# Retention and GELU MLP on one core: TensorE's order of work planned around its instruction pieces

## The chip, the core and the metric

The kernel runs on one NeuronCore of a Trainium2 chip. A core has a matrix engine (TensorE, in the profile PE, with its weight loads as PEld), a vector engine (VectorE, DVE), a scalar engine (ScalarE, ACT), GpSimd (POOL, here mostly the issuer of loads) and SyncE (SP, here the issuer of stores). Each follows its own list of instructions and waits for others by semaphores. The metric is the device time of one execution in microseconds (us); smaller is better.

## What is computed

The reference is a retention layer (attention with a decay in place of the softmax) and, on its output, an MLP with the exact GELU. Inputs are float32, the output is float32.

```python
# q, k, v: (8, 8, 576, 64)
scores = q @ k.T / sqrt(64)
gamma = 1 - 2.0 ** (-5 - arange(8))                 # one decay per head
ret = scores * where(rel >= 0, gamma ** rel, 0)     # rel = row - column
x = (ret @ v).transpose(0, 2, 1, 3).reshape(4608, 512)
h = x @ w_in                                        # w_in (512, 2048)
g = 0.5 * h * (1 + erf(h / sqrt(2)))
out = g @ w_out                                     # w_out (2048, 512)
```

## The kernel before

**Attention.** The decay lets the sequence be cut into chunks of 128 rows (the last has 64). Within a chunk the scores are computed in full and masked; what earlier chunks give comes from a running state per head, the sum of scaled keys times values. A *unit* is one chunk of one batch; there are 32 full ones and four that hold the 64-row ends of two batches each. Units 0 to 3 stand alone, later full units go two to a *group* (same chunk of two batches). For a group TensorE computes the scores (L559; L547 for units 0 to 3), VectorE masks them (L592), and then comes the *visit*: TensorE multiplies the masked scores with the values (`inner`, L646, or L631 for the short ones), updates the state (`state`, L661) and adds the state's part (`cross`, L711). Each of these is 32 small products, 64 instructions with their weight loads. VectorE scales the result and writes it to `x` (L735), which is the MLP's input. Two groups with the same chunk index can be visited together ("AA" in the loop), with 64 products each. Queries and keys of the first groups are turned by TensorE (L488, L494), later ones by VectorE (L514) with a copy by ScalarE (L525). The scaled values `vh` are made by VectorE for units 0 to 3 (L613) and by ScalarE for all others (L609, `VH_ACT`).

**MLP.** Four units make a block of 512 tokens, `t` = 0 to 8. The *first products* (x times w_in) are `mlp1` (L758): in block 0 over 128 or 256 tokens as the slices of w_in (eight, `wi0` to `wi7`) land, in block 1 over 256, then over 512. From block 6 on they are done as seven half-size products of a 2 x 2 scheme of Strassen's kind (`mlp1_fast`, L972, names "h"). The *second products* (g times w_out) are plain for half of block 0 (`mlp2`, L791) and seven half-size products for the rest (`mlp2_fast`, L862, names "f"). The sums that the schemes need are VectorE's (L817, L830, L931, L950).

**Order.** The order on each engine is written by a planner in Python when the program is built: it keeps an estimated clock `T` per engine, expected landings of loads (`sw_dma`, `share`) and times at which PSUM banks and buffers come free, and takes, in each step of its main loop (L1237 to L1345), the first due thing: a visit (A, AA), a state update (U), scores (S), a turn (T), else first or second products (`mlps`), whichever block is behind. When TensorE would wait early in the run, it issues products of zeros (`warm`, L1193). `fire` (L1156) gives VectorE, ScalarE and GpSimd their work as the clock advances: `side_jobs` holds VectorE's choices by due time, with weights such as `PER_G` and `PER_B`. `pe` (L442) advances TensorE's clock; it knows durations and changes of tiling, and nothing of how instructions arrive.

**Loads** go through one GpSimd queue in the order of the string `ORDER` (L374: `wi` and `wo` are slices of w_in and w_out, `q`, `k`, `v`, `n` those of a unit, `n` being keys in another layout, `io` the constants, `dq` a decay table) and after that by `reload`, as buffers come free. **Stores** go through SP (L1190); `STORE_AT` is when the planner thinks that block 0's begin, and `CROWD` until when it counts a store as a delay of loads.

**Names of the change.** `VISIT` and `LEAD` say from which group on, and with how much attention work ahead of the MLP, two visits are tied together (L1261); `SB` how far VectorE may be behind for scores to be issued (L1277); `AHEAD` and `RATE` how far scores run ahead of the MLP (L1221); `STATE10` from when the state of units 2 and 3 may be updated; `SLACK` how near VectorE must be to idle to get a side job.

Of the kernel before, what the change touches and what calls it, by code (L numbers as in the profile page):

```python
# [17 lines left out]
def kernel(  # L18
# [14 lines left out]
    nc = tc.nc  # L33
# [47 lines left out]
    VH_POOL = 30  # L81
# [21 lines left out]
    MSK_AT = 28.0  # L103
# [337 lines left out]

    def pe(dur, to="full"):  # L442
# [38 lines left out]
    def turn(n, jj):  # L481

        qk = loaded[groups[n][0]][0][jj]
        if n < 4:
            b, t = bank([128, HP, 128], BF16, "qk_ps")
            dst, m = turned(n, jj), HP
            for x in range(HP):
                nc.tensor.transpose(t[:, x], qk[:, 2 * x:2 * x + 2, :], ident1)  # L488
        else:
            b, t = bank([128, H, 128], BF16, "qk_ps")  # L490
            dst, m = turned(n, 1) if jj else qk.rearrange("p (h s) -> p h s", h=H), H
            for y in range(2):
                for hp in range(HP):
                    nc.tensor.transpose(t[:, y * HP + hp], qk[:, 4 * D * hp + y:4 * D * hp + 4 * D:2], ident1)  # L494
# [44 lines left out]
    def scores(n):  # L539
        g = groups[n]  # L540
        if n < 4:
            qT, kT = turned(n, 0), turned(n, 1)
            got = bank_pair(128)
            for hp in range(HP):
                for e in range(2):
                    sl = slice(64 * e, 64 * e + 64)
                    nc.tensor.matmul(got[1][:, e, hp, :], lhsT=kT[sl, hp, :], rhs=qT[sl, hp, :],  # L547
                                     start=True, stop=True)
            st[g[0]]["sc"] = got, pe(0.23, "row")
        else:  # L550
            short = len(g) == 1
            got = [bank_pair(TAIL if short else C) for _ in g]
            for hp in range(HP):
                for y in range(2):
                    for e in range(2):
                        for j in range(2):
                            sl = slice(64 * e + 32 * j, 64 * e + 32 * j + 32)
                            dst = got[0][1][64 * j:64 * j + 64, e, hp, :] if short else got[j][1][:, e, hp, :]
                            nc.tensor.matmul(dst, lhsT=turned_k(n, sl, hp, y), rhs=turned_q(n, sl, hp, y),  # L559
# [62 lines left out]
    def inner(i):  # L622
        bp, ci, j = units[i]
        s = st[i]
        if j is None:
            s["o"] = o = bank_pair(TAIL)
            for h in range(H):
                for jj in range(2):
                    sl, e = slice(64 * jj, 64 * jj + 64), 64 * (h % 2)
                    y = h // 2 + HP * (h % 2)  # L630
                    nc.tensor.matmul(o[1][e:e + 64, jj, h // 2, :], lhsT=s["vh"][sl, h, :], rhs=s["ret"][y // HP][sl, y % HP, :],  # L631
# [3 lines left out]
        else:  # L635
# [7 lines left out]
            for hp in range(HP):  # L643
                for z in range(4):
                    e, d0 = z // 2, z % 2 * 32
                    nc.tensor.matmul(o[32 * z:32 * z + 32, hp, :], lhsT=vals[:, 2 * hp + e, d0:d0 + 32], rhs=s["ret"][e][:, hp, :],  # L646
# [5 lines left out]
    def state(bp, ci):  # L652
        pair = pair_of[bp, ci]
        b, u_ps = bank([128, H, D], FP32, "u_ps")
        for hp in range(HP):
            for y in range(2):
                for e in range(2):
                    for j, i in enumerate(pair):
                        h, p0 = 2 * hp + e, 64 * e + 32 * j
                        keys = loaded[i][0][1][:, h, y::2] if i < 4 else loaded[i][2][:, j, h, y::2]  # L660
                        nc.tensor.matmul(u_ps[p0:p0 + 32, 2 * hp + y, :], lhsT=keys, rhs=st[i]["vh"][:, h, :],  # L661
# [37 lines left out]
    def cross(n):  # L699
# [6 lines left out]
        for hp in range(HP):  # L706
            for y in range(2):
                for e in range(2):
                    for j in range(2):
                        sl = slice(64 * e + 32 * j, 64 * e + 32 * j + 32)  # L710
                        nc.tensor.matmul(o[64 * e:64 * e + 64, j, hp, :], lhsT=u[sl, 2 * hp + y, :], rhs=turned_q(n, sl, hp, y),  # L711
# [42 lines left out]
    def mlp1(t, m0, n, lo, hi):  # L754
        b, hT = bank([128, n, hi - lo], FP32, "hT")
        for m in range(m0, m0 + n):
            for cc in range(N_DM):
                nc.tensor.matmul(hT[:, m - m0, :], lhsT=w_in[:, cc, m * 128:m * 128 + 128], rhs=x_tiles[t][:, cc, lo:hi],  # L758
# [26 lines left out]
    def mlp2(t, ts, m0, m1):  # L785
# [4 lines left out]
        for m in range(m0, m1):  # L790
            nc.tensor.matmul(oT, lhsT=g_of(t, ts // 2)[:, m, cols], rhs=w_out[:, m, :], start=(m == 0), stop=(m == N_DF - 1))  # L791
# [59 lines left out]
    def mlp2_fast(t, p, name):  # L851
# [9 lines left out]
        for kk in range(HK):  # L861
            nc.tensor.matmul(dst, lhsT=x[:, kk, :], rhs=y[:, kk, :], start=(name in "125" and kk == 0),  # L862
# [92 lines left out]
    def mlp1_fast(t, i, name):  # L955
# [13 lines left out]
        for m in range(2):  # L969
            for cc in range(HC):  # L970
                c0 = (2 * i + m) * 128
                nc.tensor.matmul(dst[:, m, :], lhsT=a[cc][:, c0:c0 + 128], rhs=y[:, cc, :],  # L972
# [118 lines left out]
    half = 0  # L1091
    u_due = []
# [37 lines left out]
    def side_jobs(now):  # L1130
# [12 lines left out]
        if nT in BY_DVE and nT < gA + N_TK and (half or len(apart_due) < N_TQ) and all(land.get(("qk"[half], i), 1e9) + 0.1 <= now for i in groups[nT]):  # L1143
# [49 lines left out]
    def warm(n):  # L1193
        b, t = bank([128, 512], FP32, "warm")
        for _ in range(n):
            nc.tensor.matmul(t, lhsT=zeros[:, :128], rhs=zeros, start=True, stop=True)
# [21 lines left out]
    def s_ready():  # L1218
        n = group_of[nA]
        g = groups[n]  # L1220
        if n < nT and n not in [x[0] for x in apart_due] and g[-1] // 4 <= tM1 + N_XB - 1 and nA + len(g) <= AHEAD + RATE * b1:  # L1221
# [157 lines left out]
```

## Time and profile before

| what | us |
|---|---|
| median of three runs | 292.38 (292.13 to 296.99) |
| the profiled execution: its own time | 292.46 |
| its span, first to last instruction | 290.7 |
| TensorE busy with products | 278.6 |
| VectorE, ScalarE, GpSimd busy | 228.5, 180.1, 136.0 |
| the end of block 0's first products on TensorE | 33.22 |
| first half-size first product of block 6 | 201.22 |
| TensorE's last product ends | 287.0 |

The span leaves 1.76 us of the execution outside. Rows of the profile name an engine, a line of the kernel, an operation, the tile that is written and those read, a count, busy time and the idle time before it with what ended it; "issue" means that the engine waited for nothing that the profile shows. A timeline row gives its start and its length from there; products overlap a little at their ends, so durations are best taken from start to start. The queue named "instruction" is a DMA queue, with 32 packets of 16 KB. Product records can be missing: 4155 of 4179 are there.

### The profile page before, as it was taken

What the parts mean: (1) busy time and instruction counts of PE and PEld (TensorE: products, weight loads), DVE (VectorE), ACT (ScalarE), POOL (GpSimd) and SP (SyncE); (2) the same over time, 40 slices, a digit from 0 to 9 for tenths busy, and PEclk for the clock granted to TensorE, in tenths of its full rate; (3) what the DMA queues carried; (4) which work ended last, traced back from release to release, by engine and by line L of the source; (5) the groups of instructions that cost most, each with busy time, mean ns of one, the idle gap of its engine ahead of it and who ended that gap; (6) DMA issues with size and microseconds to landing.
All of it is one profiled execution on the core that took longest, in us unless ns stands there. A gap on an engine that the chain in (4) does not pass through costs nothing.

```text
span 290.7 us, 9754 instructions
## 1 busy us (share of the span) xinstructions
PE 278.6 (96%) x4155; PEld 212.4 (73%) x4179; DVE 228.5 (79%) x380; ACT 180.1 (62%) x407; POOL 136.0 (47%) x205
## 2 busy tenths in 40 slices
PE   6999998999999999999999999999999999999994
PEld 2478766888747666665767666767888888888884
DVE  6474387896969579878996888988996998899861
ACT  7456558479779587678578596744545445555421
POOL 8956867889799777775887750000000000000000
PEclk9999999999999999999999999999999999999999
DMA  9999999999989999999999980202020202101114
GB/s 154 170 188 191 196 154 205 183 135 140 141 112 100 135 144 135 190 134 190 120 109 196 98 128 3 57 19 77 0 74 0 76 0 76 72 2 72 38 54 127
DMA packets 109131, 31.96 MB, mean 110 GB/s; under 512 B 85792, under 2 KB 104736, under 8 KB 109088
## 3 DMA queue, kind: packets, MB, share of 16 engines
q0 software_dynamic: 100400, 21.12, 83.0%
q1 hardware_dynamic: 7264, 9.51, 9.9%
q10 hardware_dynamic: 1424, 0.72, 0.9%
q8 instruction: 32, 0.52, 0.7%
q14 instruction: 11, 0.09, 0.1%
HBM read 42.99 MB, written 9.44 MB: 180 GB/s over the span
## 4 chain that ended last, share of the span: by engine, by line
PE 88%; DMA 6%; POOL 3%; issue 2%; DVE 0%; POOLq 0%
PE psum L862 36%; PE psum L758 26%; PE psum L972 13%; DMA early<-in_v_dram 3%; PE psum L559 3%; PE psum L711 3%; PE psum L646 3%; PE psum L791 2%; DMA w_in<-in_moe_w_in_dram 2%; POOL early L364 2%; PE psum L661 1%; POOL w_in L307 1%; PE psum L494 1%; PE psum L631 0%; DVE vh L613 0%
## 5 line engine op out<-in xcount | busy, mean ns | idle before, releaser
L758 PE MATMUL psum<-x,w_in 128*128 128x512 bf16 (+2 forms) x547 | 90.2, 308 | 2.7 <-issue 2.0
L758 PEld LDWEIGHTS <-w_in 128*128 128x128 bf16 x568 | 49.7, 98 | 24.1 <-issue 0.8
L862 PEld LDWEIGHTS <-g_all 128*128 128x128 bf16 x544 | 52.3, 98 | 11.4 <-issue 0.7
L763 ACT ACTIVATE g_all<-psum 128x512 bf16<-128x512 f32 x64 | 37.6, 595 | 27.3 <-PE psum L758 27.3
L862 PE MATMUL psum<-w_out,g_all 128*128 128x256 bf16 x408 | 52.0, 273 | 0.5 <-issue 0.5
L862 PEld LDWEIGHTS <-s 128*128 128x128 bf16 x408 | 39.5, 98 | 8.8
L342 POOL DMA_DIRECT2D k_ld<-in_k_dram x64 | 35.1, 569 | 21.6 <-DMA kn_ld<-in_k_dram 9.7
L609 ACT ACTIVATE vh<-v_ld,dv 128x128 bf16<-128x128 bf16 (+1 forms) x144 | 42.2, 380 | 0.0
L977 ACT ACTIVATE g_all<-t 128x512 bf16<-128x512 f32 x36 | 22.6, 630 | 29.1 <-DVE t L985 29.0
L592 DVE TENSOR_TENSOR ret<-psum,msk 128x1024 bf16<-128x1024 f32 (+1 forms) x32 | 35.7, 1150 | 4.9 <-PE psum L559 4.5
L342 POOL DMA_DIRECT2D q_ld<-in_q_dram x64 | 35.1, 568 | 2.3 <-DMA q_ld<-in_q_dram 1.4
L862 PE MATMUL psum<-wt,s 128*128 128x256 bf16 x272 | 34.1, 273 | 0.0
L848 DVE TENSOR_TENSOR o_sb<-psum,t 128x256 f32<-128x256 f32 x51 | 21.5, 421 | 13.8 <-PE psum L862 6.3
L453 ACT COPY t<-psum 128x256 f32<-128x256 f32 (+1 forms) x46 | 20.0, 434 | 17.1 <-PE psum L862 13.4
L985 DVE TENSOR_TENSOR t<-psum,t 128x512 f32<-128x512 f32 x36 | 24.7, 689 | 6.0 <-ACT t L453 4.2
L766 ACT ACTIVATE g_all<-psum 128x512 bf16<-128x512 f32 (+1 forms) x39 | 19.1, 523 | 11.2 <-PE psum L758 10.7
L972 PE MATMUL psum<-x,w_in 128*128 128x256 bf16 x192 | 25.9, 273 | 0.0
L451 DVE COPY t<-psum 128x512 f32<-128x512 f32 (+1 forms) x41 | 22.7, 559 | 3.7 <-PE psum L862 3.6
L735 DVE TENSOR_TENSOR x<-psum,dqT 128x1024 bf16<-128x1024 f32 (+1 forms) x18 | 19.3, 1099 | 2.2 <-PE psum L711 2.2
L972 PEld LDWEIGHTS <-w_in 128*128 128x128 bf16 x192 | 18.8, 98 | 2.4
L972 PE MATMUL psum<-x,ws 128*128 128x256 bf16 x144 | 19.5, 273 | 0.0
L830 DVE TENSOR_TENSOR s<-g_all 128x1024 bf16<-128x1024 bf16 x17 | 12.4, 727 | 7.4 <-ACT g_all L766 6.0
(107 smaller groups left out, 374.0 us busy)
## 6 DMA issues: line engine op xcount, KB each, us to landing
out_dram<-o_sb SPq DMA_DIRECT2D x31, 256.0 KB, 2.5
v_ld<-in_v_dram POOLq DMA_DIRECT2D x14, 256.0 KB, 5.2
q_ld<-in_q_dram POOLq DMA_DIRECT2D x48, 64.0 KB, 5.5
k_ld<-in_k_dram POOLq DMA_DIRECT2D x48, 64.0 KB, 4.5
kn_ld<-in_k_dram POOLq DMA_DIRECT2D x12, 256.0 KB, 6.5
w_in<-in_moe_w_in_dram POOLq DMA_DIRECT2D x8, 256.0 KB, 8.4
w_out<-in_moe_w_out_dram POOLq DMA_DIRECT2D x8, 256.0 KB, 9.5
q_ld<-in_q_dram POOLq DMA_DIRECT2D x4, 128.0 KB, 9.3
```

Of the source, the lines that this page charges most:

```text
L342: nc.gpsimd.dma_start(qk["qk".index(what)][p0:p0 + 32, 0:HP * per].rearrange("p (h x) -> p h x", h=HP), {"q": q, "k": k}[what][2 * bp + jj ...
L451: nc.vector.tensor_copy(dst, src)
L453: nc.scalar.copy(dst, src)
L592: nc.vector.tensor_tensor(both.rearrange("p (e h) s -> p e h s", e=2), t, by, op=ALU.mult)
L609: nc.scalar.activation(vh[:, 0:m, h], src[:, :, h], AF.Copy, scale=dv[:, h, ci:ci + 1])
L758: nc.tensor.matmul(hT[:, m - m0, :], lhsT=w_in[:, cc, m * 128:m * 128 + 128], rhs=x_tiles[t][:, cc, lo:hi], start=(cc == 0), stop=(cc == N ...
L763: nc.scalar.activation(g_all[:, t % 2, :, m0, :], hT.rearrange("p n (a c) -> p (n a) c", a=2), AF.Gelu)
L848: nc.vector.tensor_tensor(dst, src, f[key], op=ALU.add)
L862: nc.tensor.matmul(dst, lhsT=x[:, kk, :], rhs=y[:, kk, :], start=(name in "125" and kk == 0), stop=(kk == HK - 1), skip_group_check=True)
L972: nc.tensor.matmul(dst[:, m, :], lhsT=a[cc][:, c0:c0 + 128], rhs=y[:, cc, :], start=(name in "125" and m == 0 and cc == 0), stop=(cc == HC ...
L977: nc.scalar.activation(g_of(t, part)[:, m0:m0 + 2], src, AF.Gelu)
L985: nc.vector.tensor_tensor(f[key], f["b"][1], f[key], op=ALU.add)
```

## The change

TensorE's instructions are counted as they are written (`mm` and `mm_turn` stand in the place of the calls for products and turns, two instructions each). `place` says in which piece of 256 a count falls, and where in it. The planner's clock waits at the end of a piece until `FETCH`, 5 us, after the piece before was entered. `fetch_at` gives a visit or a block of scores that would cross the end of a piece the time at which the next one is expected, and the main loop doesn't take it before; two visits are tied together only if they fit into two pieces (`one_piece`). Until then other products are taken.

Products of zeros are issued until 24 us of the planner's clock, for waits over 0.5 us after 16. Half-size first products no longer ask that all groups be turned, only that all loads be issued (and, as before, that their buffers be free); turning by VectorE asks for a free buffer in the ring. Several of the planner's constants and the order of loads are other ones. `JOIN` and `JOIN_SB` are zero, so `after_a` has no effect. `VH_POOL` doesn't count in either kernel, since `VH_ACT` covers all groups from 4 on.

In the programs that are built, TensorE's products are the same but for two things: 19 products of zeros (L1196 before) for 12, and 64 products of 128 columns with 224 of 256 in blocks 0 and 1 for 112 with 200. The first products of blocks 6 to 8 and the second products from block 5 on stand in the same order. Visits stand elsewhere: that of units 8 and 9 stands ahead of seven groups of first products, a block of scores and two groups of second products that it followed before, and those of units 16 and 17 and of units 18 to 21 are no longer tied. Loads: `v3` comes two slices of w_in earlier, `q4` comes later, with two slices of w_out behind it instead of seven. SP's list of stores has the same length, and GpSimd's list the same loads.

```diff
-    AHEAD = 14
-    RATE = 3.8
-    STORE_AT = 0.0
-    CROWD = 40.0
-    STATE10 = 20.0
+    AHEAD = 13
+    RATE = 4.6
+    STORE_AT = 62.0
+    CROWD = 66.0
+    STATE10 = 32.0
     HOT = 7.5
+    FETCH = 5.0
     ARRIVE = 5.6
     WPLUS = 0
-    VISIT = 8
-    LEAD = 2.0
+    WARM_TO = 24.0
+    JOIN = 0
+    JOIN_SB = 0.0
+    VISIT = 4
+    LEAD = 5.0
     NEAR = 0.6
-    SLACK, SB, PER_G, PER_B, TURN0 = 1.2, 9.0, 6.0, 40.0, 0.0
+    SLACK, SB, PER_G, PER_B, TURN0 = 1.2, 2.0, 8.0, 20.0, 0.0
...
-    ORDER = ("wi0 io k2 q1 k1 wi7 q2 v1 k3 wi1 wo2 v0 wi6 q3 v2 wi5 wi3 wi2 v3 q4 wi4 wo1 wo0 wo4 wo7 wo6 wo3 wo5 "
-             "k4 q5 v4 k5 q6 dq2 k6 k7 q7 v6 q8 q9 k8 n4 n8 k9 q10 v8 q11 dq3 n6 k11 q12 k10 v10 n10 q13 k13 dq4 "
-             "n12 k12 v12 dq0").split()
+    ORDER = ("wi0 io q1 k2 k1 wi7 v1 q2 k3 v0 wi1 wi6 q3 wo2 v2 wi5 v3 wi3 wi4 wo1 wi2 wo3 wo0 wo4 wo5 k4 q4 wo7 "
+             "q5 wo6 v4 dq2 k5 q6 k7 k6 q7 q8 q9 n4 v6 k8 k9 v8 q10 k11 n8 n6 k10 dq3 q11 q12 v10 dq0 q13 dq4 k12 "
+             "k13 n10 n12 v12").split()
...
+    count = [3.0, 3.0]
+    piece = [0.0]
+
+    def mm(*a, **k):
+        count[0] += 2.004
+        nc.tensor.matmul(*a, **k)
...
+    def place(n):
+        return (n - 194.0) // 256, (n - 194.0) % 256
+
+    def fetch_at(n):
+
+        at = place(count[0])[1]
+        wait = piece[0] + FETCH - (256 - at) * 0.0075 if at + n >= 256 else 0.0
+        return 0.0 if T["pe"] < 20.0 else wait
+
+    def one_piece(n):
+        return place(count[0])[1] + n < 512
+
     def pe(dur, to="full"):
         if mode[0] != to:
             T["pe"] += 0.05 if mode[0][:4] == to[:4] == "row4" else 0.11
             mode[0] = to
-        T["pe"] += dur * (2.0 if T["pe"] < HOT else 1.0)
+        dur *= 2.0 if T["pe"] < HOT else 1.0
+        new, old = place(count[0])[0], place(count[1])[0]
+        if new > old:
+            turn_at = T["pe"] + dur * (1 - place(count[0])[1] / max(1.0, count[0] - count[1]))
+            wait = max(0.0, piece[0] + FETCH - turn_at) if T["pe"] > 20.0 else 0.0
+            piece[0] = turn_at + wait
+            T["pe"] += wait
+        count[1] = count[0]
+        T["pe"] += dur
         return T["pe"] + DRAIN
...
-        if ("f", t - 2, 0, "3") in waiting2 or nT < N_G or name == "7" and ("f", t - 2, 1, "4") in waiting2:
+        if ("f", t - 2, 0, "3") in waiting2 or not all_loaded() or name == "7" and ("f", t - 2, 1, "4") in waiting2:
...
-        if nT in BY_DVE and nT < gA + N_TK and (half or len(apart_due) < N_TQ) and all(land.get(("qk"[half], i), 1e9) + 0.1 <= now for i in groups[nT]):
+        if nT in BY_DVE and nT < gA + N_TK and ring_free("tk" if half else "tq") and all(land.get(("qk"[half], i), 1e9) + 0.1 <= now for i in groups[nT]):
...
-                if nA > groups[n + 1][-1]:
+                if nA > groups[n + 1][-1] and one_piece(384 if len(g) > 1 else 192):
                     both = max(ready, ready_for(n + 1))
-                    acts.append((max(both, free_time(len(g) > 1 and units[g[0]][1] < NCI - 1, out_pairs(n, n + 1))), "AA"))
+                    acts.append((max(both, fetch_at(384 if len(g) > 1 else 192), free_time(len(g) > 1 and units[g[0]][1] < NCI - 1, out_pairs(n, n + 1))), "AA"))
...
-                acts.append((max(ready, free_time(n < 4, out_pairs(n))), "A"))
+                acts.append((max(ready, fetch_at(192 if n >= 4 else 0), free_time(n < 4, out_pairs(n))), "A"))
...
-            if T["dve"] <= now + SB and nA - nB <= 2:
-                acts.append((max(s_ready(), free_time(0, len(g))), "S"))
+            if T["dve"] <= now + (SB + JOIN_SB if after_a else SB) and nA - nB <= 2:
+                acts.append((max(s_ready(JOIN if after_a else 0), fetch_at(64 if n >= 4 else 0), free_time(0, len(g))), "S"))
...
-        if now < 16 and gap > (0.6 if now < HOT else 0.2):
+        if now < WARM_TO and gap > (0.6 if now < HOT else 0.2 if now < 16 else 0.5):
```

More of the change, by code (lines that the diff above doesn't have):

```diff
@@ L80 @@
     N_KN = 4
-    VH_POOL = 30
+    VH_POOL = 16
     N_VH = 4
@@ L790, in mlp2 @@
         for m in range(m0, m1):
-            nc.tensor.matmul(oT, lhsT=g_of(t, ts // 2)[:, m, cols], rhs=w_out[:, m, :], start=(m == 0), stop=(m == N_DF - 1))
+            mm(oT, lhsT=g_of(t, ts // 2)[:, m, cols], rhs=w_out[:, m, :], start=(m == 0), stop=(m == N_DF - 1))
         done = pe((m1 - m0) * 0.2158)
@@ L1195, in warm @@
         for _ in range(n):
-            nc.tensor.matmul(t, lhsT=zeros[:, :128], rhs=zeros, start=True, stop=True)
+            mm(t, lhsT=zeros[:, :128], rhs=zeros, start=True, stop=True)
         pe((0.32 if T["pe"] < HOT else 0.2158) * n)
@@ L1233 @@
         b, t = bank([128, 512], FP32, "warm")
-        nc.tensor.matmul(t, lhsT=zeros[:, :128], rhs=zeros, start=True, stop=True)
+        mm(t, lhsT=zeros[:, :128], rhs=zeros, start=True, stop=True)
         release(b, 0.0)
@@ L1328 @@
             soon.append(v_land(nV) + 0.1)
-        if nT in BY_DVE and all(("qk"[half], i) in land for i in groups[nT]):
+        if nT in BY_DVE and ring_free("tk" if half else "tq") and all(("qk"[half], i) in land for i in groups[nT]):
             soon.append(max(T["dve"], max(land["qk"[half], i] for i in groups[nT]) + 0.1) + 0.01)
```

36 lines of the change are left out of this document (22 added, 14 removed).

## The prediction

> **What bounds the kernel now.** I read the page's busy rows first, then the chain of work that ended last, then TensorE's waits after 26 us, and last its timeline around each wait.
>
> ```profile
> PE 278.6 (96%) x4155; PEld 212.4 (73%) x4179; DVE 228.5 (79%) x380; ACT 180.1 (62%) x407; POOL 136.0 (47%) x205
> PE   6999998999999999999999999999999999999994
> q8 instruction: 32, 0.52, 0.7%
> ```
>
> TensorE is busy in every slice but the first and the last. [...] The chain, in order of time, splits the run:
>
> ```profile
> 8.69 6.54 DMA w_in<-in_moe_w_in_dram
> 15.51 9.76 DMA early<-in_v_dram
> 25.30 0.70 DVE vh L613
> 26.46 6.92 PE psum L758 x96
> ```
>
> Until 26 us the chain is loads; the last is the values of unit 3, landed at 25.27. From 26.46 it is TensorE almost alone. What it still waits for after 26 us:
>
> ```profile
> PE psum L758 <- issue: 2.0, 8, 0.5
> PE psum L711 <- issue: 1.4, 1, 1.4
> PE psum L862 <- issue: 0.5, 1, 0.5
> PE psum L661 <- DVE vh L613: 0.3, 1, 0.3
> ```
>
> So after 26 us no engine and no load holds TensorE up: "issue" is all. 24 product records are missing (4155 against 4179 weight loads), and a missing record looks like a 0.16 us gap, so I compared each run of products with its own rate (128 columns 0.056, 256 columns 0.109, 512 columns 0.216 us each). Four real stops are left: 1.65 us in the L711 run at 47.84, 0.59 in the L758 run at 78.96, 0.65 in the L862 run at 140.34, 0.74 in the L758 run at 164.11: **3.6 us**. Two of them:
>
> ```profile
> 47.84 0.35 PE L711 MATMUL psum<-q_ld,u_sb 32*64 32x128 bf16 x10
> 49.60 0.52 PE L711 MATMUL psum<-q_ld,u_sb 32*64 32x128 bf16 x22 [1.41 <-issue]
> ...
> 140.34 1.38 PE L862 MATMUL psum<-w_out,g_all 128*128 128x256 bf16 x11
> 142.19 0.70 PE L862 MATMUL psum<-w_out,g_all 128*128 128x256 bf16 x5 [0.48 <-issue]
> ```
>
> They cut a run in two at a place where no operand changes. Counting weight loads and products, they stop at instruction 1215, 2493, 4793 and 5561, and 194 + 256 x (4, 9, 18, 21) is 1218, 2498, 4802, 5570. In the trace's packet records the last instruction packet before each stop landed at 48.13, 78.17, 140.79 and 163.85; products resumed at 49.60, 79.90, 142.19 and 165.40, 1.4 to 1.7 us later. So a stop is a piece that isn't there. Each packet starts after TensorE enters the piece before it, 0.5 to 4.0 us later while loads run (0.85 to 1.0 us of transfer), which makes the time from entering one piece to being able to enter the next 2.6 to 6.2 us over the 22 pieces between 43 and 190 us, median 3.9, over 5 us in six.
>
> [...]
>
> **The change part by part.** The built programs' orders are known, so I can place each product.
>
> Pieces. TensorE's time from one boundary to the next follows from rows: 32 products of scores 0.56 us, inner 0.46, state 0.35, cross 0.57; in pairs (64) as here:
>
> ```profile
> 137.79 1.08 PE L646 MATMUL psum<-ret,vh 128*32 128x128 bf16 x64
> 138.69 0.70 PE L661 MATMUL psum<-vh,kn_ld 128*32 128x64 bf16 x64
> 139.32 1.08 PE L711 MATMUL psum<-q_ld,u_sb 32*64 32x128 bf16 x64
> ```
>
> that is 0.90, 0.63 and 1.02 from start to start. Before, the short pieces take 2.8, 3.8, 4.0, 4.0, 4.0, 4.2, 4.3, 4.9, 4.9, 5.4, 5.5, 5.6 us. In the new order they take 4.7, 4.9, 4.9, 5.1, 5.1, 5.3, and nine of 5.5 to 5.9: fewer products of visits stand in one piece, because the new count and test (lines 447 to 484 of the changed kernel) put a visit just behind a boundary, and MLP products between. Laying the 22 measured fetch times over the pieces of before, place by place, gives 4.5 us of stops where 3.6 were measured (0.8 of it); over the new pieces 2.4, so 1.9 with that factor. Drawing them at random gives 5.3 before (0.67) and 1.9 after, so 1.3. I take **1.6 us of stops, a gain of 2.0**; ends: none left (gain 3.6), and 3.6 as before (gain 0). A visit that waits costs TensorE nothing by itself: behind the tests stand first and second products, which are the same in sum, and no visit of before was waited for.
>
> Visits alone. VISIT 4 and LEAD 5 join other visits than before: those of units 16/17 and of 18 to 21 were joined and are now single. A single visit takes 0.46 + 0.35 + 0.57 = 1.38 us, a joined one 2.55 for two: **+0.25** for the two splits with the short one at the smaller sizes (bounds 0 and 0.4).
>
> The first 40 us. Seven more products of zeros (19 against 12) and another order of loads. What one costs:
>
> ```profile
> 9.76 1.06 PE L1196 MATMUL psum<-zeros 128*128 128x512 bf16 x2
> 14.56 0.59 PE L1196 MATMUL psum<-zeros 128*128 128x512 bf16 x2
> ```
>
> About 0.45 us each at 9.76 and 0.22 at 14.56, though the granted clock reads 1.00 for the whole stretch. [...] Up to the first full-width first product there are 15 zeros against 12; walking the new order from 5.5 us with these rates I reach it near 17.1 instead of 16.44. Then landings: loads land in order, 1.3 us for a slice of w_in or w_out, 0.9 for one of q, k, v, so unit 3's values, two slices of w_in earlier, land near 22.6 instead of 25.27, and the last slice of w_in near 28.2 (27.86, less q4's 0.9, plus a slice of w_out). TensorE's own work from 17.1 to the end of block 0's first products adds to 33.5 us; the landing bound (28.2 + 0.1 + 4.0 us of products left) is 32.3; before it was 33.22, with 0.35 us of state work already done that the new order has still to do. Against before that is 0.63 lost by TensorE's walk and 0.57 gained by the landings alone. The last slice of w_out lands near 38.3 instead of 36.6, just before its use near 38.5 to 39.6. So this part lies between 0.6 gained and 1.75 lost (one more zero at 0.45, six at 0.22, all on the path). The later of the two bounds decides, so I take **+0.4**, nearer to the walk, and a little less since some zeros may run at the faster rate.
>
> At nothing: half-size first products as soon as buffers are free (line 1047 of the changed kernel): they still start behind the last first product of block 5 and in the same order, so buffers were not what they waited for. Fewer, wider products in block 0 (48 of 128 columns become 24 of 256) 0.06. VH_POOL: all scaled values from unit 4 on are ScalarE's (L83) in both. STORE_AT and CROWD tell the planner when stores collide with loads; SP has only stores to issue and takes them when data is ready (41.0 us), so the real collision stays. The new ring test for DVE's turns changes which job is next at 79% busy; cover is the 20% idle, and TensorE waited for DVE once in 0.3 us. Unit 8's visit comes near 61.5 instead of 71.04; its values landed at 56.46 and scaling them takes 2.44, so 2.5 us are to spare even at the old landing.
>
> Sum against the profiled execution, 292.46 us (span 290.7 and 1.76 around it; the runs' median is 292.38): 292.46 - 2.0 + 0.25 + 0.4 = **291.1**.
>
> **Rivals.**
> - The pieces come in time everywhere and the early order is bound by landings: 292.46 - 3.6 + 0.25 - 0.6 = **288.5**. For: no new interval is under 4.7 and the median fetch is 3.9. Against: six of 22 took over 5.
> - The stops are not what the order can move: 3.6 stays, 292.46 + 0.25 + 0.4 = **293.1**. For: fetches were slowest (5.7 to 6.2) at 142 to 163 us, where loads run after a visit, and visits still end in loads. Against: the stops sit at block ends. [...]
> - Slower: zeros on the path. At 8 to 20 us, between the turns and visits of units 0 to 3, TensorE works in order, so seven more zeros delay all behind them, 1.75 us; with stops of 2.4 left, 292.46 - 1.2 + 0.25 + 1.75 = **293.3**. It decides from the point where block 0's first products are bound by TensorE (last one later than 33.9 us) and not by landings. For: from 26.46 on TensorE hardly idles, so what is lost is not regained. Against: the last slice of w_in holds it to 32.3 anyway, so 0.6 us of zeros are free.
> - Late data: the planner believes stores at 62 us that come at 41 to 55, and has put unit 8's visit 9 us earlier. If its values or keys land after 59 us, TensorE waits: 1 us each; three make **294.1**. Against: the 2.5 us to spare.
>
> **How the numbers follow.** Forecast 0.45 (289.7 to 292.3); pieces in time 0.20 (287.6 to 289.7); stops unmoved 0.13; zeros 0.12; late data 0.10. The range 288.2 to 293.8 leaves out late data and the lower part of the second case. Two per cent (about what a measurement of this kernel can tell from no change) is 286.5 to 298.2: faster 0.03, same 0.92, slower 0.05. All gains I can find add to 4.2 us, under the 5.8 that 2% needs.
>
> **What would show it.** Stops at block ends after 40 us: 1 to 2.5 us in sum, none over 1.2. Block 0's last first product ending between 32.3 and 33.9 us. The half-size products (x with w_in, 256 columns, after block 5) starting near 200.0 instead of 201.4. Wrong, if TensorE waits for a DMA, DVE or ACT after 42 us, or if the visits' runs are longer than 1.4 and 2.6 us.

## The result and the profile after

The changed kernel takes 291.02 us (median of 13 runs, 290.07 to 292.22) against 292.85 us for the kernel before beside it (13 runs): ratio 0.995, interval 0.9929 to 0.9971. That is 1.5 us less by the ratio and 1.8 by the medians, well within 2%. Two runs of the kernel before, at 296.3 and 297.0 us, were in a slower state, and the ratio leaves them out. The forecast was 291.1, which is 1.4 less than the 292.46 of the profiled execution.

The profiled execution of the changed kernel took 290.48 us, its span 288.7. In the changed kernel all products are recorded under one line, L452 (`mm`), and turns under L456 (`mm_turn`), so what was L646, L661, L711, L758 or L862 is now told apart by its tiles. First the page of the changed kernel: busy times, TensorE over 40 slices, the instruction queue.

```profile
PE 279.1 (97%) x4138; PEld 212.5 (74%) x4162; DVE 229.5 (80%) x384; ACT 178.8 (62%) x400; POOL 136.2 (47%) x205
PE   6899999999999999999999999999999999999994
q8 instruction: 32, 0.52, 0.7%
```

TensorE's busy time is 0.5 us larger (it has seven products of zeros more), while the span is 2.0 us smaller: TensorE stands still for 2.5 us less. The chain of work that ended last, start, length and what:

```profile
2.52 5.81 DMA early<-in_q_dram
...
21.59 12.01 PE psum L452 x140
...
47.60 0.38 ACT t L489
...
48.02 12.08 PE psum L452 x326
```

The loads of w_in and v that carried the chain from 8.69 to 25.27 before are no longer on it: from 8.4 us on TensorE's own work carries it, but for two copies of VectorE near 20 us and one of ScalarE at 47.60. TensorE's waits after 26 us (what for, us in total, times, longest):

```profile
PE psum L452 <- issue: 0.8, 5, 0.2
PE psum L452 <- ACT t L489: 0.5, 1, 0.5
```

Before, "issue" stood at 3.9 us on three lines with a longest of 1.4. What is left of it is five pieces of at most 0.2, which is what missing records look like (24 are missing). Against their own rates the runs of products show one stop at the end of a piece, 0.14 us, in the third run of the visit below (instruction 1218). A new wait, for ScalarE, stands ahead of that visit. The timeline of TensorE (start, length, line, operation, output and inputs, count, idle time before):

```profile
46.52 1.04 PE L452 MATMUL psum<-w_out,g_all 128*128 128x256 bf16 x8
48.02 1.03 PE L452 MATMUL psum<-wt,g_all 128*128 128x256 bf16 x8 [0.46 <-ACT t L489]
48.98 0.63 PE L452 MATMUL psum<-ret,vh 128*32 128x128 bf16 x32
49.44 0.42 PE L452 MATMUL psum<-vh,k_ld 128*32 128x64 bf16 x32
49.79 0.74 PE L452 MATMUL psum<-q_ld,u_sb 32*64 32x128 bf16 x32
...
198.26 2.77 PE L452 MATMUL psum<-x,w_in 128*128 128x512 bf16 x20
```

In the last row the run of 512-column products passes into the half-size ones after four of 0.216 us: they begin at 199.13, where before they began at 201.22. So the whole 2.1 us is won before 200 us, and from there both kernels run alike: TensorE's last product ends at 284.9 against 287.0.

### The profile page after: what moved, and what is told of

Its sections match the earlier page's. It is cut to its first block, busy times and chain, and to the rows that moved or that the text cites. A ratio compares the mean times of both kernels' runs of the same rounds, so it can differ in the third digit from the quotient of the medians.

```text
span 288.7 us, 9727 instructions
## 1 busy us (share of the span) xinstructions
PE 279.1 (97%) x4138; PEld 212.5 (74%) x4162; DVE 229.5 (80%) x384; ACT 178.8 (62%) x400; POOL 136.2 (47%) x205
## 4 chain that ended last, share of the span: by engine, by line
PE 95%; DMA 2%; issue 1%; DVE 0%; POOL 0%; ACT 0%; POOLq 0%; DVEq 0%
PE psum L452 93%; DMA early<-in_q_dram 2%; PE psum L456 1%; POOL w_in L311 0%; DVE qkT L487 0%; DVE o_sb L884 0%; ACT t L489 0%; POOL val L188 0%; POOLq L188 0%; DVEq L487 0%; POOLq L1404 0%; POOL pos L190 0%
## 5 line engine op out<-in xcount | busy, mean ns | idle before, releaser
L452 PE MATMUL psum<-x,w_in 128*128 128x256 bf16 (+2 forms) x716 | 116.8, 303 | 1.6 <-issue 0.8
L452 PEld LDWEIGHTS <-w_in 128*128 128x128 bf16 x736 | 68.1, 98 | 26.1 <-issue 0.3
L452 PEld LDWEIGHTS <-g_all 128*128 128x128 bf16 x576 | 55.6, 98 | 15.1 <-issue 0.6
L452 PE MATMUL psum<-w_out,g_all 128*128 128x256 bf16 (+1 forms) x438 | 58.6, 280 | 0.0
L452 PEld LDWEIGHTS <-s 128*128 128x128 bf16 x408 | 39.3, 98 | 8.5
L1013 ACT ACTIVATE g_all<-t 128x512 bf16<-128x512 f32 x36 | 22.6, 630 | 29.0 <-DVE t L1021 28.9
L452 PE MATMUL psum<-wt,s 128*128 128x256 bf16 x272 | 34.3, 273 | 0.0
L487 DVE COPY t<-psum 128x512 f32<-128x512 f32 (+1 forms) x41 | 22.6, 558 | 2.9 <-PE psum L452 2.9
L452 PE MATMUL psum<-x,ws 128*128 128x256 bf16 x144 | 19.5, 273 | 0.0
L357 POOL DMA_DIRECT2D v_ld<-in_v_dram x14 | 16.3, 1167 | 4.0 <-ACT g_all L799 2.0
L452 PE MATMUL psum<-wt,g_all 128*128 128x256 bf16 x136 | 17.5, 273 | 0.5 <-ACT t L489 0.5
L452 PE MATMUL psum<-w_out,s 128*128 128x256 bf16 x136 | 17.5, 273 | 0.0
```

The source lines that it names most:

```text
L452: nc.tensor.matmul(*a, **k)
L487: nc.vector.tensor_copy(dst, src)
L1013: nc.scalar.activation(g_of(t, part)[:, m0:m0 + 2], src, AF.Gelu)
```

## The experiments

### Do pieces of 256 instructions stop TensorE, and does their place decide it?

The theory says that a stop is an instruction piece that has not arrived, so the same work in the same order, moved against the ends of pieces, should cost another time. The rival says that the stops belong to the work (its loads, its visits) and not to the ends. The plainest test moves everything in the kernel before by 48 instructions: 24 products of eight columns, behind the first seven zeros, in an early wait.

```diff
     release(b, 0.0)
+    b, t = bank([128, 512], FP32, "warm")
+    for _ in range(24):
+        nc.tensor.matmul(t[:, 0:8], lhsT=zeros[:, :128], rhs=zeros[:, 0:8], start=True, stop=True)
+    release(b, 0.0)
```

> The kernel before, with 24 products of zeros of 8 columns behind the first seven, while TensorE waits for its first data. Nothing else is moved; every later instruction of TensorE stands 48 places further on, so the ends of its pieces of 256 fall elsewhere in the work. Theory (a stop is a piece that isn't there yet): the stops still come at instructions 194 + 256 n, which are other places of the work, and the work between ends is now as short as 1.7, 1.9, 2.0 and 2.1 us in four pieces; laid against the fetch times measured before (2.6 to 6.2 us) that gives 11 us, with the factor of 0.67 to 0.8 some 7 to 9 us of stops in place of 3.6, and 296 to 298 us. Rival (the stops belong to places of the work, such as the cross products of units 4 and 5): they stay where they were, 3.6 us, and the time is that of before, 292 to 293.5.

Measured: 299.81 us (297.45 to 301.74), ratio 1.0228, interval 1.0177 to 1.0279: 6.7 us slower. The turning of k4 and k5, a mark at the end of the loads' part, begins at 41.72 against 41.44, so in these two profiles 0.3 us of the difference lies in the early stretch. TensorE's waits of this kernel after 26 us:

```profile
PE psum L758 <- issue: 3.7, 8, 1.8
PE psum L711 <- issue: 2.7, 1, 2.7
PE psum L862 <- issue: 1.8, 1, 1.8
```

No engine and no load is named, as before, but "issue" is 8.2 us. Two places of its timeline:

```profile
56.63 0.39 PE L758 MATMUL psum<-x,w_in 128*128 128x256 bf16 x2
58.78 3.57 PE L758 MATMUL psum<-x,w_in 128*128 128x256 bf16 x16 [1.76 <-issue]
...
140.99 0.92 PE L711 MATMUL psum<-q_ld,u_sb 32*64 32x128 bf16 x51
144.60 0.58 PE L711 MATMUL psum<-q_ld,u_sb 32*64 32x128 bf16 x13 [2.70 <-issue]
145.12 3.08 PE L862 MATMUL psum<-w_out,g_all 128*128 128x256 bf16 x16
```

Both stops cut a run in which no operand changes. Against the rates of the runs there are four stops, of 1.9, 2.9, 1.2 and 2.0 us, 8.0 in sum against 3.6. They stand at instructions 1725, 4793, 5561 and 6327: the ends 1730, 4802, 5570 and 6338 are 194 + 256 x (6, 18, 21, 24), so the ends stayed where they were and other work came to stand across them.

What follows the first two stops is slow as well. The 16 products at 58.78 take 3.57 us and the 16 at 145.12 take 2.91 to the next row, where 16 at 0.109 are 1.75: in the trace's clock record (a list of stretches, each with the share of the clock that was granted) the clock is half for 3.41 us from 58.78 and again from 144.11, and 1.00 next to these stretches. That is 3.2 us more, which the expectation didn't have. The 4.4 us of added stops, the half clock and the early 0.3 make 7.9 of the 9.3 us between the two profiled executions (301.74 and 292.46); the rest is not traced. The theory holds in the stops (7 to 9 us expected), the time is over its 296 to 298, and the rival falls.

The same from the other side: in the changed kernel `place` counts from a wrong origin, half a piece off, so that the planner waits by the same rule, but for ends that aren't there.

```diff
-        return (n - 194.0) // 256, (n - 194.0) % 256
+        return (n - 66.0) // 256, (n - 66.0) % 256
```

> The changed kernel, with the planner's ends of pieces put half a piece off (66 in place of 194). Visits and scores wait as they did, for an end that is in the wrong place; constants, zeros and loads are those of the changed kernel. Theory: what helps is the place of a visit against the real end. The pieces' work is then as short as 1.6, 1.7 and 4.0 us, 7 to 9 us by the fetch times of before, 5 to 6.5 with the factor: 295.5 to 297.5. Rival (the constants, the loads or fewer visits in a row made the gain, the place doesn't matter): 290.5 to 292.

Measured: 298.5 us (298.17 to 299.77), ratio 1.0195, interval 1.0159 to 1.0231: 7.5 us over the changed kernel, a little more than the theory's upper end. Its waits after 26 us, and one of its stops:

```profile
PE psum L452 <- issue: 5.5, 8, 1.8
PE psum L452 <- ACT t L489: 0.7, 1, 0.7
```

```profile
172.02 0.81 PE L452 MATMUL psum<-q_ld,u_sb 32*64 32x128 bf16 x44
174.67 0.47 PE L452 MATMUL psum<-q_ld,u_sb 32*64 32x128 bf16 x20 [1.85 <-issue]
```

Here the large stops are at instructions 1215, 5561 and 6329, at ends again. With a smaller one at 4793 they add to 5.6 us, of 8.3 by which this execution (298.82 us) is longer than the profiled one of the changed kernel; the granted clock is 1.00 throughout, and of the rest only 0.7 us in the first 42 and a wait for ScalarE that is 0.2 longer are traced. So it is not the waiting that helps, but waiting for the right place.

### What does the waiting bring by itself?

With `FETCH` at zero the planner of the changed kernel believes that pieces are always there; everything else stays.

```diff
-    FETCH = 5.0
+    FETCH = 0.0
```

> The changed kernel with FETCH at 0 in place of 5: no visit and no block of scores waits for a piece, and the planner's clock has no stops; two visits are still tied only if they fit into two pieces. Theory: stops come back, 4.7 to 5.7 us by the fetch times of before, 3.2 to 4.5 with the factor, where the changed kernel shows 0.1: 294 to 295.5. Rival (the other constants and the loads made the gain): 290.5 to 292.

Measured: 293.54 us (291.6 to 296.51, 10 runs), ratio 1.001, interval 0.9982 to 1.0038. That is 2.5 us over the changed kernel by the medians and 1.8 by the ratios, under the theory's 294 to 295.5 and over the rival's 290.5 to 292. In its profile (296.51 us, the longest of the ten) the stops are back at ends, 2.5 us at instruction 1215 and 0.6 at 5303, and the granted clock is half for 3.41 us from 52.06, as TensorE resumes behind the first. Taken out of the changed kernel, the waits are worth 1.8 to 2.5 us, against a gain of 2.0 in the forecast.

Then the other way round: the changed code with the constants and the order of loads of before, so that counting and waiting are nearly all that is new (the two changed tests, for half-size products and for turns by VectorE, stay).

```diff
...
-    AHEAD = 13
+    AHEAD = 14
...
-    WARM_TO = 24.0
+    WARM_TO = 16.0
...
-    VISIT = 4
-    LEAD = 5.0
+    VISIT = 8
+    LEAD = 2.0
...
-    ORDER = ("wi0 io q1 k2 k1 wi7 v1 q2 k3 v0 wi1 wi6 q3 wo2 v2 wi5 v3 wi3 wi4 wo1 wi2 wo3 wo0 wo4 wo5 k4 q4 wo7 "
...
+    ORDER = ("wi0 io k2 q1 k1 wi7 q2 v1 k3 wi1 wo2 v0 wi6 q3 v2 wi5 wi3 wi2 v3 q4 wi4 wo1 wo0 wo4 wo7 wo6 wo3 wo5 "
...
```

> The changed kernel's code with the constants, the order of loads and the rule for zeros of the kernel before: of the change only the count of pieces, the waits of visits and scores for them and the two ring tests are left. The pieces' work is then 3.5, 4.0, 4.5, 4.8 and more, 2.4 to 3.2 us of stops by the fetch times of before, 1.6 to 2.3 with the factor, and the first 42 us are those of before (the turn of k4 and k5 at 41.4, not 41.9). Theory (the pieces make the gain, the new loads and zeros cost 0.4 to 0.5): 1.3 to 2.0 us under before, about as fast as the changed kernel. Rival (loads, zeros and constants make the gain): the time of before within 0.5 us.

Measured: 292.13 us (290.79 to 294.02), ratio 0.9964, interval 0.9937 to 0.9992: 1.05 us won where 1.3 to 2.0 were expected. Its profile has no stop of 0.6 us or more at an end; TensorE's waits after 26 us, and the larger one:

```profile
PE psum L452 <- DVE x L771: 0.9, 1, 0.9
PE psum L452 <- DVE kT L487: 0.3, 1, 0.3
```

```profile
53.31 1.92 PE L452 MATMUL psum<-x,w_in 128*128 128x256 bf16 x16 [0.85 <-DVE x L771]
```

The stops are gone, and a third of what they cost (1.2 of 3.6 us) has come back as waits for VectorE: the visit that ends at 51.41 gives the `x` that the products at 53.31 read, and only eight second products, 0.95 us, stand between them. The remaining 0.5 to 0.8 us would be the constants' and the order of loads', but the intervals of the two kernels overlap (0.9937 to 0.9992 here, 0.9929 to 0.9971 there), so that share isn't established.

### Are the order of loads and the zeros needed?

> The changed kernel with the order of loads of before, and zeros up to 16 us of the planner's clock as before (12 of them behind the first seven); all other constants and the waits are the changed kernel's. The planner then orders visits anew: the pieces' work is 3.2, 4.0, 4.9 and more, 3.3 to 3.9 us of stops by the fetch times of before, 2.2 to 2.9 with the factor. Theory (new loads and zeros cost 0.4 to 0.5 us at the turn of k4 and k5): that turn comes at 41.4 again, stops are 2 us longer than the changed kernel's, and the time is 1 to 2 us over it. Rival (the new loads and zeros are a gain of their own): over 2.5 us longer.

This is the changed kernel with the `ORDER` of before and `WARM_TO` at 16 (those lines of the diff above, alone). Measured: 292.69 us (291.47 to 293.47), ratio 0.999, interval 0.9964 to 1.0016; by the time 1.7 us over the changed kernel, as the theory had it. But the reason is not the expected one alone. Its waits and one place:

```profile
PE psum L452 <- issue: 1.4, 2, 1.3
PE psum L452 <- ACT g_all L802: 0.9, 1, 0.9
PE psum L452 <- DVE x L771: 0.5, 1, 0.5
PE psum L452 <- DVE kT L487: 0.3, 1, 0.3
PE psum L452 <- ACT g_all L799: 0.3, 1, 0.3
```

```profile
56.65 2.79 PE L452 MATMUL psum<-x,w_in 128*128 128x256 bf16 x24
60.36 1.03 PE L452 MATMUL psum<-x,w_in 128*128 128x256 bf16 x8 [0.92 <-ACT g_all L802]
```

One stop of 1.4 us, at instruction 5303, is there although the planner waited 5 us, and 2.0 us of waits for ScalarE and VectorE beside it. The longest of these, at 60.36, isn't a late piece: it stands 23 instructions ahead of the end 1730, where the stops stand 3 to 13 ahead of theirs, the last instruction packet had landed 2.6 us earlier (1.4 to 1.7 at the stops of the kernel before), and ScalarE ends its reading of the bank at 60.31. I took it for a stop, and let the kernel wait 6 us (`FETCH = 6.0`), expecting the stops to go and the time to fall to 290 to 291:

> As the run with the old order of loads and zeros, with FETCH 6 in place of 5 us. The pieces' work is then 4.2, 4.8, 5.0 and seven of 5.7 to 6.3: 1.1 us of stops by the fetch times of before, under 1 with the factor. Theory (stops and the early part add up, and 6 us covers nearly all fetches): the turn of k4 and k5 at 41.4, stops under 1 us, 0.3 to 1 us faster than the changed kernel, 290 to 291. Rival (waiting longer takes the work that other waits need, so that TensorE waits for ScalarE or VectorE instead): over 1 us of such waits, and 291 to 293.

Measured: 294.39 us (293.49 to 295.53), ratio 1.0059, interval 1.0035 to 1.0082: slower, against the theory. Waits after 26 us and the place:

```profile
PE psum L452 <- DVE x L771: 2.2, 1, 2.2
PE psum L452 <- DVE ret L628: 0.5, 1, 0.5
PE psum L452 <- DVE kT L487: 0.3, 1, 0.3
```

```profile
51.79 0.64 PE L452 MATMUL psum<-q_ld,u_sb 32*64 32x128 bf16 x32
54.63 1.58 PE L452 MATMUL psum<-x,w_in 128*128 128x256 bf16 x13 [2.20 <-DVE x L771]
```

No stop of 0.3 us or more is left at an end, and it is the slowest of the three: the visit that ends at 52.36 now stands right ahead of the products that read its `x`, with nothing between, and TensorE waits 2.2 us for VectorE. So longer waits can cost more than they save. How much of the 1.7 us they cost here is open: in this profile the first 42 us alone took 1.5 us longer than in the profile with 5 us (42.60 against 41.10 at the turning of k4 and k5). Whether 6 us would also lose with the new order of loads was not tried.

For the zeros, the changed kernel with each of its 19 made of eight columns instead of 512 (same count, same order, so no end of a piece moves):

```diff
-            mm(t, lhsT=zeros[:, :128], rhs=zeros, start=True, stop=True)
+            mm(t[:, 0:8], lhsT=zeros[:, :128], rhs=zeros[:, 0:8], start=True, stop=True)
```

> The changed kernel, with the 19 products of zeros after the first seven cut from 512 to 8 columns; their number, the order of everything and the planner's clock are the same, so that only the time of the zeros goes. Theory (zeros are on the path, bound by the landing of the last slice of w_in at 28.2): block 0's first products end 0.3 to 0.9 us earlier than at 33.22, the turn of k4 and k5 comes nearer to their landing at 40.8, and the run is 0.2 to 0.6 us shorter. Rival (the zeros keep the clock up, or fill waits only): the first products of 8 to 20 us run slower, and the time is the same or up to 1 us longer.

Measured: 291.5 us (290.29 to 292.06, 12 runs), ratio 0.9935, interval 0.9914 to 0.9955; the changed kernel has 0.995. No difference can be told. In stretches of this kernel's early part the columns are window, length, busy time and count of each engine, granted clock, DMA share, GB/s:

```profile
8.00:12.00 4.00, 2.59 (x43) 2.03 (x44) 2.61 (x5) 1.42 (x3) 3.88 (x6) 0.55 2.10 169
12.00:16.00 4.00, 3.60 (x71) 2.75 (x72) 2.85 (x5) 1.55 (x3) 3.40 (x5) 0.50 1.79 182
16.00:18.00 2.00, 2.00 (x17) 1.12 (x14) 0.42 (x1) 1.03 (x2) 1.28 (x3) 0.50 1.73 189
18.00:20.00 2.00, 2.00 (x18) 1.67 (x17) 1.29 (x2) 0.75 (x2) 0.60 (x1) 0.84 1.83 177
```

The granted clock is half until past 18 us: eight first products of 256 columns take 1.87 us at 15.65, where the changed kernel needs 1.04 at 16.25. TensorE spends 3.3 us less on zeros between 8.8 and 14.7 us (0.27, 0.26 and 0.29 from start to start for the three groups, against 2.70, 0.52 and 0.86 in the changed kernel) and loses it again to the half clock and to waits for loads. The zeros bring about what they cost.

### The new wait for ScalarE

The forecast was to be wrong if TensorE waits for ScalarE after 42 us, and it does, 0.5 us at 47.6: second products of block 0's second half (those of the scheme's product "4") stand in front of the waiting visit, and they wait for ScalarE to copy the product before them ("7"). If that wait is a cost of its own, leaving the copy out (the sum reads the copy before it, so a part of the output is another) saves 0.5 us; if it only stands where the piece at instruction 1218 would be late anyway, nothing.

```diff
+        if key == "t3" and f is fast.get((0, 1)):
+            f[key] = f["t2"]
+            f[key + "at"] = on("act", 0.34, f["adone"]) + SEM
+            return
```

> The changed kernel without ScalarE's copy of the partial sum behind the seventh product (name 7) of the second half of block 0; the sum that needs it reads the copy behind the sixth in its place, so that part of the output isn't the reference's. Everything else stands in the same order. In the changed kernel TensorE waits 0.46 us for that copy at 47.6, and its next end of a piece (instruction 1218) comes 1.9 us later with a stop of 0.14 us. Theory (the copy's wait lies in front of a piece that is late anyway, so it costs nothing): the wait goes, the stop at 1218 grows by about as much, to some 0.5 us, and the time is the same within 0.2 us. Rival (the wait is a cost of its own): 0.5 us shorter.

Measured: 290.98 us (289.8 to 292.28), ratio 0.9932, interval 0.9901 to 0.9964, against 291.02: nothing by the medians. The ratio is 0.0018 lower than the changed kernel's 0.995, 0.5 us, well inside both intervals, so the time alone can't tell the two answers apart. Its timeline at the visit:

```profile
49.91 0.47 PE L452 MATMUL psum<-q_ld,u_sb 32*64 32x128 bf16 x19
50.90 0.38 PE L452 MATMUL psum<-q_ld,u_sb 32*64 32x128 bf16 x13 [0.53 <-issue]
```

The wait for ScalarE is gone, and the stop at 1218 has grown from 0.14 to 0.78 us. In this profile the wait had taken the place of a stop.

### Both kernels once more

One profile shows one execution, and the stops vary. So both kernels were profiled a second time.

> The changed kernel once more, for the scatter of one profile: by the theory that loads and zeros cost 0.4 us in the first 42 us, the turn of k4 and k5 comes at 41.9 again, later than in before; if the difference of the first 42 us is scatter, it comes anywhere between 41 and 42.6, the values of the four kernels with the old loads.

> The kernel before once more, for the same reason: by the theory the turn of k4 and k5 comes at 41.4 again and the stops at instructions 1218, 2498, 4802 and 5570 add to 3.0 to 4.2 us; if the early difference is scatter, the turn lies anywhere between 41 and 42.6, and if the stops depend on the loads' luck their sum differs by over 1 us or they come at other ends of pieces.

Measured, one execution each: 293.11 us for the changed kernel, 293.3 for the one before. In this second profile of the changed kernel (line numbers one less) two of four stops:

```profile
57.04 0.35 PE L451 MATMUL psum<-ret,vh 128*32 128x128 bf16 x11
57.88 0.51 PE L451 MATMUL psum<-ret,vh 128*32 128x128 bf16 x21 [0.50 <-issue]
...
101.15 0.19 PE L451 MATMUL psum<-q_ld,kT 32*64 32x64 bf16 x1
101.78 0.44 PE L451 MATMUL psum<-q_ld,kT 32*64 32x64 bf16 x31 [0.44 <-DMA k_ld<-in_k_dram]
```

The profile names a load of keys at 101.78, but that landed at 101.35, while the place is the end 3266 and the instruction packet landed 1.5 us before TensorE resumed, as at the other stops. With 0.38 at instruction 1218 and 0.46 at the end 5570 (168.40) they add to 2.15 us, where the first profile had 0.14. In the kernel before, the second profile has about 3.1 to 3.3 us where the first had 3.6; the largest is again at instruction 1215, with about 1.4 us. So in these pairs of profiles the ends are the same (in the kernel before even the four that stop it), and what each costs is not. This one execution of the changed kernel lies above all 13 timed ones; the 1.5 to 1.8 us rest on the timed runs, not on a pair of profiles.

## Why the prediction was right, and where not

**The bound.** That after 26 us only the arrival of TensorE's instructions holds it up, in stops at instruction 194 + 256 n, is shown: 48 instructions more cost 6.7 us (in the profile, about a third of the added time is the clock that fell behind two of the stops), and waiting for ends half a piece off 7.5 us. The 256 is read from the runs: the four stops of before lie 1278, 2300 and 768 instructions apart, within 4 of 5, 9 and 3 times 256, and the page of before has 32 packets of 16 KB for TensorE's 4179 weight loads and as many products. Most ends (the prediction's "block ends") cost little: four of the 32 pieces stop TensorE by 0.3 us or more, in the kernel before and in the shifted one. But these few are 3.6 us of the kernel before, and 8.0 of the shifted one with 3.2 of half clock behind two of them. The rival of stops that the order can't move falls. One reading of the prediction was too narrow: over its 22 pieces the packets took 0.9 to 1.4 us, not 0.85 to 1.0; the sum doesn't use it.

**Stops, 3.6 to 1.6, a gain of 2.0.** Taken out of the changed kernel the waits are worth 1.8 to 2.5 us (`FETCH` at zero), put into the kernel before they win 1.05; so the term's sign and order of size are right. The 1.6 that should be left was met by no profile: 0.14, 0.78 and 2.15 us in three (the middle one without the copy), 1.0 on average. I had laid measured fetch times over the new pieces as if the intervals between ends alone decided; that gives no scatter, and the scatter between executions is as large as the term. The faster rival, all pieces in time, describes the first profile (0.14) and not the other two, and its 288.5 was not reached by any run. Of the signs given for it, "none over 1.2" held in all three, the sum of 1 to 2.5 in one, and the half-size products began at 199.13 where 200.0 was forecast, and at 200.18 and 201.72 in the other two.

**Visits alone, +0.25.** No run tested it by itself. The visit's runs have the lengths of before (0.46, 0.35 and 0.57 to 0.67 us from start to start in the rows at 48.98), so a single visit still takes 1.4.

**The first 40 us, +0.4.** In the profiled pair it came as predicted: the turning of k4 and k5 begins at 41.90 against 41.44, 0.46 later. Block 0's first products end near 33.2 in both, inside the 32.3 to 33.9 of the forecast, and the landings fit (unit 3's values 22.56 for 22.6, the last slice of w_in 28.20 for 28.2). But over more profiles this mark scatters by 1.5 us, and the clock record of the traces orders it. With the old order of loads and few zeros it stands at 41.10, 41.44 and 41.72 in three profiles (the shifted kernel among them), and at 42.53, 42.58 and 42.60 in three in which the granted clock fell to half for 3.41 us near 20 us. There TensorE had just waited 2.0 to 2.2 us for a slice of w_in, as in the second profile of the kernel before:

```profile
19.16 1.82 PE L757 MATMUL psum<-x,w_in 128*128 128x256 bf16 x8 [2.12 <-DMA w_in<-in_moe_w_in_dram]
```

With the new order and its zeros TensorE has no such wait, and no profile shows that fall; the mark follows the time at which the full clock is first recorded: 41.90 with 12.15 us, 42.55 to 42.64 with 13.40 to 13.64 (the kernel waiting at a shifted place among them). The first profile of the kernel before had the full clock from 13.60 and no fall, at 41.44, so at like clock the new early order is slower by 1.1 us, and against an execution with the fall it is level. The 0.4 is near the difference of the means, 42.42 less 42.00, but as a term it came out by luck, as far as single profiles tell: TensorE's walk costs more than the 0.63 of the prediction, and a fall of the clock that the forecast didn't know slows the old order by as much in half of its profiles. The slower rival, zeros on the path, said that seven more zeros delay all behind them by 1.75 us; with the zeros' time taken away nothing is won, and in that run the clock rises late, at 18.65 us, against 12.15. That reason falls: it priced the zeros and not the products behind them: eight of 256 columns take 1.87 us in that run and 1.04 in the changed kernel.

**At nothing.** Half-size products as soon as buffers are free, `VH_POOL`, the planner's store times: the order of the built programs doesn't show them at work, and the profile shows nothing to add. Unit 8's visit, 9 us earlier, waits for no load; the rival of late data didn't come about.

**What I had at nothing and wasn't.** "Behind the tests stand first and second products, which are the same in sum" holds for the sum, but not for what they need: products taken ahead of a waiting visit can want data that isn't there. Here this gave 0.5 us of wait for ScalarE, which by the profile without the copy took the place of a stop, since the piece at 1218 was late as well. With other constants it gave 1.2 us (counting and waiting alone), 2.0 (the old order of loads) and 3.0 (the same, waiting 6 us). The first and the last had no large stop left; the first still won only 1.05 us, and the last was 1.7 us slower than with 5 us.

**The sum.** From the profiled 292.46: -3.5 for the stops (3.6 to 0.14), +0.5 for ScalarE, +0.46 for the first 42 us and +0.25 for single visits as estimated make 290.2, and 290.48 was measured. That the forecast of 291.1 lies within 0.1 us of the median of the runs, 291.02, is luck in part: stops of 1.0 on average are 0.6 under its 1.6, the wait for ScalarE of 0.5 was not in it, and the early part came out by the clock.

## What to carry to other kernels

Where one engine issues hundreds of short instructions, read gaps marked "issue" inside a run of equal products, count instructions from the start, and see whether the gaps sit a fixed number apart. Here they sat at the ends 194 + 256 n, the arrival of instructions was the limit, and 24 tiny products ahead of the work moved the time by 2%. Put longer instructions between dense stretches so that none spans a whole piece within the fetch time (here 2.6 to 6.2 us in the kernel before), and no more than that: with the old order of loads and `FETCH` at 6 in place of 5 the large stops were gone, TensorE waited 2.2 us for VectorE instead, and the time was 1.7 us longer. Where products behind a gap take longer than their rate, look at the granted clock before that time is counted as part of the stop (16 products took 3.57 us at half clock where their rate gives 1.75). One profile of such a kernel is not enough, since the same kernel had 0.14 us of stops in one execution and 2.15 in another.

## What the runs showed that I had not expected

Twenty-four products of eight columns, hidden in an early wait, cost 6.7 us of 293 with the order of all other work unchanged, part of it by the clock that fell behind two of the stops.

In six places of the traces the granted clock falls to half for 3.41 us about when TensorE resumes (from 0.5 us before to 1.3 after): behind the three waits of 2.0 to 2.2 us for w_in named above, and behind stops of 1.9, 2.5 and 2.9 us. Two stops of 2.0 us and one wait of 2.2 us for VectorE (at 54.63 with `FETCH` at 6) passed without it. So the length alone doesn't decide, and what does, no run here tells.

Early on, the granted clock in the views and the durations seem to disagree: the views read 1.00 from the start, and yet in the changed kernel six products of zeros take 2.77 us at 8.77, some 0.45 each where 0.216 is the full rate. The reason is that the trace's clock record has no entry before 12.15 us there, or before 13.60 in the kernel before, and the views count what has no entry as 1.00; from the first entry on the products have the full rate (in the kernel before eight of 128 columns take 0.46 us at 13.66, against 0.45 by the rate of 0.056). That is also why the prediction read 1.00 for the whole stretch. Where the record starts is no fixed point of a kernel: two profiles of the kernel before have it at 13.60 and 9.03.

The instruction packets start up to 4.3 us after TensorE enters the piece before, and not only while loads run. The last load lands at 174.3 us in the kernel before, 170.9 in the changed one, 173.9 in the shifted one and 174.5 in the one that waits at a shifted place, and in the last two TensorE still stops for 2.0 us at 190.4 and for 1.6 at 197.6. From 203 us on, where a piece takes 14 us, the packets of both kernels start with TensorE's entry into a piece or up to 1.8 us ahead of it, and no stop at an end was found. Why a packet starts when it does was not tried; the loads alone can't be the reason.
